# Two transfers, of 120 and of 8 partitions, in place of one of 128 for each quarter of the first weight matrix

## The chip, the cores and the metric

The kernel runs on one core of a Trainium2 chip. The metric is the device time of one execution in microseconds (us); the median of the runs of a kernel counts. Before the change three runs are there: 278.73, 279.89 and 282.72 us, median 279.89 us.

## What is computed

Causal retention with a decay per head, over 8 batches, 8 heads, 576 positions and a head size of 64; its output, laid out as 4608 tokens by 512, goes through two dense layers with a leaky ReLU between them.

```python
scores = scale * np.matmul(q, k.transpose(0, 1, 3, 2))
Dmat = np.where(rel >= 0, gamma[:, None, None] ** rel[None, :, :], 0.0)
attn_out = np.matmul(scores * Dmat[None, :, :, :], v)
x = attn_out.transpose(0, 2, 1, 3).reshape(4608, 512)
h = x @ w_in                      # 512 x 2048
g = np.maximum(0.01 * h, h)
out = g @ w_out                   # 2048 x 512
```

Inputs and output are float32.

## The kernel before, in words

**Units and groups.** The 4608 tokens are 36 units of 128 tokens (two chunks of 64 positions each), and four units make a group of 512 tokens, nine groups in all. Retention is done in chunks: inside a chunk by a masked product, across chunks by a running state per head.

**Names of the steps.** For unit u, `ld u.1`, `ld u.0` and `ld u.2` load k, q and v (line 340, tile `t`); a unit in which a batch ends is loaded by two transfers of 64 partitions each in place of one of 128. `ck`, `cq` and `cv` cast them to float16, q and v with the decay factors (lines 365 and 369). `tp` turns q and k on TensorE for the first eight units (L405) and `yt` copies them out (L412). `sa` and `sb` are the score and state products (L439, L448), `mk` the mask (L454), `st` the running state (L479 to L485), `sx` its float16 copy (L497, L500), `oa` or `ca`/`ow` the output products (L536), and `x u` copies the result into the group's `xT` (L585).

**The dense layers.** For groups 0 and 1 the first layer is done by plain products `h g.f0.t0` (L634: weights from `w_in`, moving data from `xT`), whose results pass through the leaky ReLU on ScalarE (`l`, L641). For the later groups both layers use seven products in place of eight on 2 by 2 blocks (L823 and L901), with sums of weight blocks (`ws`, L709, and `wm`, L680) and of activations made on VectorE. The stage of L634 runs until about 64 us of the span; after that nearly all of the time is the seven products.

**Weights.** `w_in16` is a float16 tile of 128 partitions by 4 by 2048. `load_w_in(f)`, line 602, loads quarter f (512 of the 2048 columns, all four blocks of 128 rows) with one transfer on the POOL queue, line 606, which casts float32 to float16 on the way: 128 partitions by 4 rows of 512 elements. `w_out16` is loaded by four such transfers, line 615. A product `h0.f0.t0` needs only the quarter that holds its columns: f0 = 0 to 3 need quarter 0, 4 to 7 quarter 1, 8 to 11 quarter 2, 12 to 15 quarter 3. The weight sums `ws` need all four quarters.

**What sets the order.** One string, `ORDER`, lists every step of the program; each engine and each queue carries out its own steps in that order. All loads up to unit 11, except k and q of unit 0, go through POOL, and so do the eight weight loads, so that they share one queue. Around the change the order of POOL's loads is (from `ORDER`, only the `ld`, `wi` and `wo` words):

```
ld2.1 ld3.0 ld3.1 wi0 ld4.0 ld3.2 wi1 ld4.1 ld5.1 ld4.2 ld5.2 wi2 ld6.2 ld5.0 ld6.1 wi3 ld7.2 ld7.1 ld8.1
ld6.0 ld8.2 ld7.0 ld9.1 ld9.2 wo0 wo2 wo1 wo3
```

Unit 4 is one that is loaded in halves, so `ld4.0`, `ld4.1` and `ld4.2` are two transfers each. The input tiles have four buffers for each of q, k and v. Words such as `+5@0` are products on an idle tile (L973) that keep TensorE going in the first 20 us.

Of the kernel before, what the change touches and what calls it, by code (L numbers as in the profile page):

```python
# [33 lines left out]
class Plan:  # L34
# [3 lines left out]
    def add(self, name, eng, run, after=(), opens=(), uses=(), mode="f"):  # L38
        j = Job(name, eng, run, [a for a in after if a is not None], list(opens), list(opens) + list(uses), mode)
        assert name not in self.jobs  # L40
        self.jobs[name] = j
        return j
# [169 lines left out]
def kernel(  # L212
# [9 lines left out]
    nc = tc.nc  # L222
# [2 lines left out]
    DFF = moe_w_in.shape[1]  # L225
    P = 128
    CH = 64
    BLK = 256
    NP = H // 2
    NF = DFF // P  # L230
# [2 lines left out]
    NU = NT // P  # L233
    CB = S // CH
    HF, HN, HT = NF // 2, DM // 2, TOK // 2
# [6 lines left out]
    def place(c):  # L242
        return (c % CB) % (BLK // CH)

    kinds = sorted({(place(2 * n), place(2 * n + 1)) for n in range(NU)})
    tab = np.zeros((P, len(kinds), 2, H))
    for w, at in enumerate(kinds):
        r = np.concatenate([CH * a + np.arange(CH) for a in at])[:, None] - BLK / 2
        tab[:, w, 0] = gamma[None, :] ** r * scale
        tab[:, w, 1] = gamma[None, :] ** (-r)  # L250
    s_idx = np.arange(P) % CH
    mask = (np.arange(CH)[None, :] >= s_idx[:, None]).astype(np.float32)
    gblk = np.zeros((P, NP))
    for p in range(NP):
        for g in range(2):
            gblk[CH * g : CH * g + CH, p] = gamma[p + NP * g] ** BLK
    consts = np.concatenate([tab.reshape(P, -1), mask, gblk], axis=1).astype(np.float32)
# [32 lines left out]
    w_in16 = const_pool.tile([P, NP, DFF], F16, name="w_in16")  # L290
# [138 lines left out]
    def inner(u):  # L429
# [39 lines left out]
        for j in range(2):  # L469
            if not live(u, j):  # L470
                carry[0] = None
                continue
            scaled = (2 * u + j) % CB % (BLK // CH) == BLK // CH - 1
            before = carry[0]
# [127 lines left out]
    def load_w_in(f):  # L602
        fs = slice(f * FQ, (f + 1) * FQ)

        def run():
            nc.gpsimd.dma_start(  # L606
                out=w_in16[:, :, fs], in_=moe_w_in.rearrange("(c k) f -> k c f", k=P)[:, :, fs]
            )

        w_in_job[f] = add(f"wi{f}", "POOL", run)  # L610
        follow(w_in_job[f])
# [365 lines left out]
    def follow(j):  # L977
        j.follow = last.get(j.eng)
        last[j.eng] = j
# [65 lines left out]
```

## Time and profile before

| what | value |
|---|---|
| median of 3 runs | 279.89 us (278.73 to 282.72) |
| the profiled execution's own time | 278.81 us |
| its span, first to last instruction | 277.0 us |
| mean granted TensorE clock | 0.997 of full speed |
| PE matmul, weight load, DVE, ACT, POOL busy | 97%, 81%, 84%, 70%, 14% |
| HBM read, written | 36.81 MB, 9.44 MB |

The profile is one execution. Its page gives the busy time of each engine (PE is the matrix engine, PEld its weight loads, DVE the vector engine, ACT the scalar engine, POOL the engine whose queue carries the casting transfers, SP the queue of the other transfers); the other views used are the timeline of one engine, the table of stretches with the busy time of each engine in each, the list of who waited for whom, the chain of work that ended last, and the view of one source line in a stretch, whose last row gives the time from the start of an issue to the landing of the data. In a timeline row stand the start, the length, the engine, the line, the operation with its tiles, the count, and in brackets the idle time of the engine before it with what ended it.

### The profile page before, as it was taken

How to read it: one execution, taken by the hardware profiler on the slowest of the kernel's cores; microseconds unless marked ns; L12 is line 12 of the kernel's file. 1: busy time of each engine (PE TensorE's matmuls, PEld its weight loads, DVE VectorE, ACT ScalarE, POOL GpSimd, SP SyncE). 2: the span in 40 equal slices, each digit the busy share in tenths (PEclk: the TensorE clock that was granted, in tenths of full speed). 3: DMA queues.
4: the chain of work that ended last, by engine and by line, in shares of the span. 5: the costliest groups of instructions: out<-in, count | busy, mean ns of one | idle time of the engine just before them, and what ended most of it. 6: DMA issues, size and time to landing. Idle time of an engine off the chain costs nothing.

```text
span 277.0 us, 10028 instructions
## 1 busy us (share of the span) xinstructions
PE 268.8 (97%) x4329; PEld 225.3 (81%) x4329; DVE 232.0 (84%) x438; ACT 195.2 (70%) x411; POOL 38.1 (14%) x49
## 2 busy tenths in 40 slices
PE   6999999999999999999999999999999999999994
PEld 2468668888888888888888888888898888888883
DVE  3888698979998999999989998999989968775650
ACT  2354596698889998798787889796769455447620
POOL 8958792200000000000000000000000000000000
PEclk9999999999999999999999999999999999999998
DMA  7999999987999999999999999998913700400404
GB/s 217 264 249 247 254 268 215 304 175 165 238 230 216 233 220 234 206 227 207 225 203 215 235 213 237 183 243 202 162 40 124 108 2 2 154 0 0 154 2 153
DMA packets 119597, 50.05 MB, mean 181 GB/s; under 512 B 107904, under 2 KB 113280, under 8 KB 119552
## 3 DMA queue, kind: packets, MB, share of 16 engines
q1 hardware_dynamic: 111984, 35.99, 60.3%
q0 software_dynamic: 6992, 13.11, 19.5%
q8 instruction: 34, 0.56, 0.8%
q10 hardware_dynamic: 576, 0.31, 0.4%
q14 instruction: 11, 0.09, 0.1%
HBM read 36.81 MB, written 9.44 MB: 167 GB/s over the span
## 4 chain that ended last, share of the span: by engine, by line
PE 88%; DMA 5%; POOL 3%; DVE 2%; issue 1%; ACT 0%; ACTq 0%; POOLq 0%; DVEq 0%
PE acc L901 40%; PE acc L823 31%; PE acc L634 9%; PE ot L536 4%; DMA t<-in_k_dram 3%; POOL t L340 2%; PE sc L448 2%; DMA t<-in_q_dram 2%; PE sc L439 2%; POOL w_in L606 1%; DVE osb L940 0%; PE acc L405 0%; DVE sum L847 0%; ACT acc L765 0%; DVE xT L585 0%
## 5 line engine op out<-in xcount | busy, mean ns | idle before, releaser
L901 PEld LDWEIGHTS <-gt 128*128 128x128 f16 x720 | 69.9, 98 | 8.3
L901 PE MATMUL acc<-w_out,gt 128*128 128x256 f16 x432 | 53.6, 273 | 0.0
L823 PEld LDWEIGHTS <-w_in 128*128 128x128 f16 x448 | 42.6, 98 | 5.8 <-issue 0.3
L843 ACT ACTIVATE gt<-acc 128x512 f16<-128x512 f32 x56 | 33.3, 601 | 13.7 <-PE acc L823 13.3
L901 PE MATMUL acc<-w_mix,gt 128*128 128x256 f16 x288 | 36.3, 273 | 0.0
L823 PEld LDWEIGHTS <-w_sum 128*128 128x128 f16 x336 | 32.3, 98 | 4.0
L851 ACT ACTIVATE gt<-sum 128x512 f16<-128x512 f32 x56 | 34.4, 635 | 1.1 <-DVE sum L847 0.9
L823 PE MATMUL acc<-xs,w_in 128*128 128x256 f16 x224 | 33.4, 273 | 0.3 <-ACT gt L843 0.3
L823 PE MATMUL acc<-xT,w_in 128*128 128x256 f16 x224 | 33.7, 273 | 0.0
L823 PE MATMUL acc<-xs,w_sum 128*128 128x256 f16 x224 | 33.7, 273 | 0.0
L901 PEld LDWEIGHTS <-mix 128*128 128x128 f16 x288 | 28.0, 98 | 3.8 <-DVE mix L877 0.4
L634 PE MATMUL acc<-xT,w_in 128*128 128x256 f16 (+2 forms) x272 | 30.3, 266 | 0.4 <-DVE xT L585 0.3
L454 DVE TENSOR_TENSOR s<-sc,cs 128x512 f16<-128x512 f32 x36 | 24.7, 685 | 5.7 <-PE sc L439 3.9
L634 PEld LDWEIGHTS <-w_in 128*128 128x128 f16 x272 | 22.0, 98 | 6.0 <-DMA w_in<-in_moe_w_in_dram 0.6
L641 ACT ACTIVATE gt<-acc 128x512 f16<-128x512 f32 x32 | 18.2, 599 | 10.2 <-PE acc L634 10.2
L762 ACT COPY acc<-acc 128x512 f32<-128x512 f32 x33 | 19.0, 577 | 8.8 <-PE acc L901 4.1
L847 DVE TENSOR_TENSOR sum<-acc,k 128x512 f32<-128x512 f32 x28 | 19.2, 688 | 6.6 <-ACT k L776 3.5
L369 DVE TENSOR_TENSOR qk<-t,cs 128x512 f16<-128x512 f32 x32 | 21.9, 683 | 1.0 <-DMA t<-in_q_dram 1.0
L585 ACT CAST xT<-ot 128x512 f16<-128x512 f32 x29 | 16.9, 591 | 8.1 <-PE ot L536 8.0
L776 ACT COPY k<-acc 128x512 f32<-128x512 f32 x31 | 18.3, 589 | 6.0 <-PE acc L823 3.6
L369 DVE TENSOR_TENSOR v<-t,cs 128x512 f16<-128x512 f32 x31 | 21.1, 684 | 0.4 <-PE ot L536 0.3
L847 DVE TENSOR_TENSOR sum<-acc,u 128x512 f32<-128x512 f32 x28 | 19.2, 686 | 2.4 <-PE acc L823 1.2
(64 smaller groups left out, 429.0 us busy)
## 6 DMA issues: line engine op xcount, KB each, us to landing
out_dram<-osb SPq DMA_DIRECT2D x16, 512.0 KB, 4.6
t<-in_k_dram SPq DMA_DIRECT2D x22, 256.0 KB, 4.3
t<-in_q_dram SPq DMA_DIRECT2D x22, 256.0 KB, 4.5
t<-in_v_dram SPq DMA_DIRECT2D x21, 256.0 KB, 4.0
t<-in_v_dram POOLq DMA_DIRECT2D x11, 256.0 KB, 5.9
t<-in_k_dram POOLq DMA_DIRECT2D x10, 256.0 KB, 8.1
t<-in_q_dram POOLq DMA_DIRECT2D x10, 256.0 KB, 6.5
w_in<-in_moe_w_in_dram POOLq DMA_DIRECT2D x4, 512.0 KB, 8.4
```

Of the source, the lines that this page charges most:

```text
L369: engine[e].tensor_tensor(out=view[0](out), in0=view[1](t32[u, 2 * x][:]), in1=view[1](decay(u, x)), op=MUL)
L454: landed[u] = nc.vector.tensor_tensor(out=s[:], in0=sc[:, :, 0], in1=mask_sb.unsqueeze(1).unsqueeze(1).to_broadcast([P, 2, NP, CH]), op=MUL,)
L585: moved[u] = copies[xe](out=x_of(u).rearrange("q c (j t) -> q j c t", j=2), in_=at)
L634: nc.tensor.matmul(out=a[:, n, :], lhsT=w_in16[:, c, (f0 + n) * P : (f0 + n + 1) * P], rhs=x[:, c, t0 : t0 + nt], start=(n == 0 and c == 0 ...
L641: nc.scalar.activation(out=y[:, f0 : f0 + nf, t0 : t0 + nt], in_=a[:], func=mybir.ActivationFunctionType.Lrelu)
L762: copies[ce](out=B[:], in_=A[:])
L776: op("k5", ke, lambda: copies[ke](out=k5[:], in_=C[:]), [done["5"]], [k5], [C])
L823: nc.tensor.matmul(out=r[:, f, :], lhsT=w[:, c, (2 * n + f) * P : (2 * n + f + 1) * P], rhs=rhs[:, c, :], start=fresh and c == 0 and f == ...
L843: w = op(what, "ACT", lambda: nc.scalar.activation(out=to(), in_=r[:], func=lr), after, [y], [r])
L847: what, "DVE", lambda: nc.vector.tensor_tensor(out=s[:], in0=r[:], in1=plus[:], op=ADD),
L851: f"l{g}.{n}.{what}", "ACT", lambda: nc.scalar.activation(out=to(), in_=s[:], func=lr), [j], [y],
L901: nc.tensor.matmul(out=(r[tb] if isinstance(r, tuple) else r)[:, tb, :], lhsT=lhs[n]()[:, f, tb * P : (tb + 1) * P], rhs=rhs[n][:, f, :], ...
```

## The change

`PW = 120` is added, and `load_w_in` issues two transfers in place of one, the first for partitions 0 to 119 and the second for partitions 120 to 127. Both stay on the POOL queue, next to each other, at the place in `ORDER` where the one stood. The steps that need a quarter need both of its parts. `load_w_out` stays as it is.

```diff
     P = 128
     CH = 64
+    PW = 120
...
         def run():
-            nc.gpsimd.dma_start(
-                out=w_in16[:, :, fs], in_=moe_w_in.rearrange("(c k) f -> k c f", k=P)[:, :, fs]
-            )
+            for ps in (slice(0, PW), slice(PW, P)):
+                nc.gpsimd.dma_start(
+                    out=w_in16[ps, :, fs], in_=moe_w_in.rearrange("(c k) f -> k c f", k=P)[ps, :, fs]
+                )
```

## The prediction, made before the changed kernel was run

> **What bounds the kernel now.** I read the page first, then the table of stretches, then the chain that ended last, then the queues that feed its start.
>
> ```profile
> span 277.0 us, 10028 instructions
> PE 268.8 (97%) x4329; PEld 225.3 (81%) x4329; DVE 232.0 (84%) x438; ACT 195.2 (70%) x411; POOL 38.1 (14%) x49
> ```
>
> TensorE is busy for 97% of the span. The question is where the remaining 3% lies and whether the loading of w_in has to do with it. Columns of the next table: stretch, its length, busy time of PE, PEld, DVE, ACT and POOL with counts, granted clock, mean busy share of the DMA engines, GB/s.
>
> ```profile
> 10.00:15.00 5.00, 4.86 (x79) 2.29 (x74) 4.82 (x10) 1.70 (x4) 5.00 (x8) 1.00 1.00 225
> 15.00:20.00 5.00, 4.71 (x119) 2.93 (x117) 4.28 (x11) 2.37 (x6) 2.08 (x4) 1.00 1.12 244
> 20.00:25.00 5.00, 4.89 (x130) 4.39 (x124) 3.43 (x8) 2.52 (x6) 3.85 (x5) 1.00 1.07 236
> 25.00:30.00 5.00, 4.56 (x103) 3.60 (x98) 3.73 (x9) 2.58 (x5) 5.00 (x7) 1.00 1.08 239
> 30.00:35.00 5.00, 5.00 (x91) 3.20 (x90) 3.90 (x9) 2.84 (x6) 3.11 (x5) 1.00 1.08 291
> 35.00:60.00 25.00, 25.00 (x363) 20.54 (x361) 23.11 (x44) 18.89 (x42) 10.08 (x12) 1.00 1.11 247
> ```
>
> From 30 to 60 us PE has no idle time. From 10 to 30 us, while the quarters of w_in are loaded, it lacks 0.14 + 0.29 + 0.11 + 0.44 = 0.98 us. That is the most that any faster loading of w_in can give back. The DMA share is 1.00 or more all the way (packets overlap), so the transfers run behind each other without a gap. Now the end of the start-up, from the chain of work that ended last, and the two places where PE's weight loads waited:
>
> ```profile
> 13.86 8.95 DMA t<-in_k_dram
> 25.86 0.69 DVE xT L585
> 26.61 1.96 PE acc L634 x32
> ```
> ```profile
> 18.42 0.91 PEld L634 LDWEIGHTS <-w_in 128*128 128x128 f16 x16 [0.61 <-DMA w_in<-in_moe_w_in_dram]
> 26.60 1.79 PEld L634 LDWEIGHTS <-w_in 128*128 128x128 f16 x32 [0.40 <-DVE xT L585]
> ```
> ```profile
> 22.90 0.76 DVE L365 CAST qk<-t 128x512 f16<-128x512 f32 x1 [0.98 <-DMA t<-in_k_dram]
> 23.91 0.65 DVE L365 CAST qk<-t 128x512 f16<-128x512 f32 x1
> ```
>
> The first wait is for quarter 0 itself. The second comes from the second half of k of unit 4, issued at 13.86 and landed at about 22.8: DVE stood 0.98 us before the cast at 22.90, and the copy x3 that PE needed at 26.60 is behind that cast on DVE. So two landings matter at first: quarter 0 at 18, k of unit 4 at 22.8. How POOL issues these:
>
> ```profile
> 9.30 0.77 POOL L606 DMA_DIRECT2D w_in<-in_moe_w_in_dram  x1
> 10.05 1.39 POOL L340 DMA_DIRECT2D t<-in_q_dram  x2
> 11.43 0.99 POOL L340 DMA_DIRECT2D t<-in_v_dram  x1
> 12.41 0.77 POOL L606 DMA_DIRECT2D w_in<-in_moe_w_in_dram  x1
> 13.16 2.28 POOL L340 DMA_DIRECT2D t<-in_k_dram  x3
> 18.36 2.26 POOL L340 DMA_DIRECT2D t<-in_v_dram  x3 [2.92 <-DMA w_in<-in_moe_w_in_dram]
> 20.61 0.77 POOL L606 DMA_DIRECT2D w_in<-in_moe_w_in_dram  x1
> 22.54 0.89 POOL L340 DMA_DIRECT2D t<-in_v_dram  x1 [1.15 <-DMA w_in<-in_moe_w_in_dram]
> ```
>
> Count the transfers between a quarter and the load that waits for it, although that load has nothing to do with w_in. After 9.30 come 2 + 1 + 1 + 3 = 7, and the eighth, at 18.36, waits. After 12.41 come 3 + 3 + 1 = 7, and the eighth, at 22.54, waits. I read this as a rotation: POOL's queue has eight transfers open, and the n-th waits until the one eight places before it has landed. The landings, from the views of the two lines in short stretches (quarters 0, 1, 2, then the second half of k4 with k5):
>
> ```profile
> L606 POOL DMA_DIRECT2D w_in<-in_moe_w_in_dram x1: 767/767/767, 9.3 to 9.3; - x1
> DMA to landing us min/median/max: 8.5/8.5/8.5
> ```
> ```profile
> L606 POOL DMA_DIRECT2D w_in<-in_moe_w_in_dram x1: 772/772/772, 12.4 to 12.4; - x1
> DMA to landing us min/median/max: 9.6/9.6/9.6
> ```
> ```profile
> L606 POOL DMA_DIRECT2D w_in<-in_moe_w_in_dram x1: 772/772/772, 20.6 to 20.6; - x1
> DMA to landing us min/median/max: 6.8/6.8/6.8
> ```
> ```profile
> L340 POOL DMA_DIRECT2D t<-in_k_dram x2: 697/799/901, 13.9 to 14.5; - x2
> DMA to landing us min/median/max: 8.9/9.1/9.3
> ```
>
> Quarter 0 lands at 9.30 + 8.5 = 17.8, quarter 1 at 22.0, quarter 2 at 27.4, k4's second half at 13.86 + 8.9 = 22.8, k5 at 14.5 + 9.3 = 23.8. Each waiting load starts 0.5 to 0.6 us after its landing (18.36 after 17.8, 22.54 after 22.0).
>
> **The change part by part.** *The issue.* Four more instructions stand on POOL. An 8-partition issue is not in the trace. The rows nearest to it are the 64-partition loads, 1.39 us for two (0.70 each), the 128-partition loads, 0.89 (2.26 for two halves and a whole), and w_in, 0.77. Carried on to 8 partitions on the line through the first two it is 0.70 - 56 x 0.19 / 64 = 0.53 us, which I take. It cannot be under zero, since the queue is in order and the issue takes time; its upper bound is the 0.77 of a whole quarter. Four cost +2.1 us of POOL (0 to 3.1); the 120-partition issue saves next to nothing. What hides it: POOL stands 2.92 and 1.15 us in the rows above, and the DMA engines are busy throughout. Without that cover two issues ahead of k4 would be +1.1 us. On the path: 0.
>
> *The packets.* The same bytes move. Their pace is seen while quarter 3 moves, from 28.7 to 30.9 us:
>
> ```profile
> DMA packets 353, 0.38 MB, mean 171 GB/s; under 512 B 3, under 2 KB 347, under 8 KB 353
> ```
>
> 353 packets in 2.2 us are 160 per us; a quarter has 128 x 4 = 512, so 3.2 us, or 32 packets of 0.10 us on each of 16 engines. If 120 partitions go 8 to an engine, fifteen engines get the same 32 and one gets none; the other 8 partitions are 32 packets more, 4 each if they spread over eight engines (+0.4 us there), or 3.2 us if one engine takes them (the engine left free, or one that then has 64). Bounds of quarter 0's landing: below, an engine that now ends late is freed; above, +0.4. A delay of 0.4 at 18.42 is swallowed by the 0.40 for which PE stands at 26.60. I take 0.
>
> The Trainium skill, "DMA: Bandwidth & Descriptors", section "Rules for kernel authors", speaks against such a split: two transfers of disjoint partitions use the same engines and serialize, so one of 128 is better. By it the sum would be that of one issue more and no gain, 0 to +0.4 here; the trace agrees so far that transfers queue behind each other (DMA share 1.00 to 1.12).
>
> *The rotation.* This is what the change moves. Quarter 0 takes two of the eight places, quarter 1 two as well. Counting again: q4 (two), v3, quarter 1 (two) and the first half of k4 follow quarter 0's small part; the second half of k4 is then the eighth after quarter 0's large part, and waits for it. It is issued at about 17.8 + 0.56 = 18.4 in place of 13.86, and k5 behind it at 19.1. Both were 8.9 and 9.3 us under way only because quarters were ahead. What a load needs with little ahead of it:
>
> ```profile
> t<-in_v_dram POOLq DMA_DIRECT2D x3, 256.0 KB, 4.4
> t<-in_k_dram POOLq DMA_DIRECT2D x3, 256.0 KB, 4.6
> t<-in_q_dram POOLq DMA_DIRECT2D x3, 256.0 KB, 4.2
> ```
>
> (medians of the loads issued before 9 us). So k4 lands between 18.4 + 4.2 = 22.6 and, with 4.6 and the 0.4 of packets, 23.4; now 22.8. k5: 19.1 + 4.2 to 5.0 = 23.3 to 24.1; now 23.8. I take no shift, because quarter 1 is still ahead and lands at 22.0. Quarter 2 is next: its large part stands eight places behind quarter 1's large part, so it starts at 22.0 + 0.56 = 22.6 in place of 20.61. With the same 6.8 it would land at 29.4; but part of the 6.8 was the queue, and v5, issued about 0.7 later than now, ends at about 25.7, which puts quarter 2 (2.5 us behind it now: 27.4 against 19.7 + 5.2) at 28.2 to 28.6. PE first uses it here:
>
> ```profile
> 28.94 2.76 PE L634 MATMUL acc<-xT,w_in 128*128 128x512 f16 x12
> ```
>
> That leaves 28.94 - 0.56 = 28.4 as its due time: from no cost to 29.4 - 28.4 = +1.0; I take 0, as it just fits.
>
> *Sum.* 0 + 0 + 0 against the profiled execution's 278.81 us (span 277.0 and 1.8 around it). That one lies 1.1 below the median of the runs shown, 279.89; on the median the forecast is **279.9 us**.
>
> **The rivals.**
>
> *A late engine is relieved.* A quarter has landed when the last engine is done. No view shows the engines apart. If the engine that carries partitions 120 to 127 is the one that ends late, it loses 32 packets, 3.2 us, per quarter, and quarter 0, k4 and k5 land earlier together. For it: 3.2 us of packets against landings of 6.8 to 9.6 leave room for an uneven end. Against it: the queue explains that too. Price: at most PE's 0.98 us, so 278.9. The Trainium skill's same page, section "Latency and other measured facts", says that engines 7 and 15 are usually slower, with a cause that it calls a best guess, and its section "Why a DMA increments its semaphore by 16 and not by 1" would put 120 partitions on engines 0 to 14 and so free 15. By these two the result would be this rival's 278.9; the trace can neither confirm nor deny which engine is late, so the chance stays small.
>
> *The rotation starves the engines: slower.* With k4's second half issued at 18.4, k5 at 19.1 and quarter 2 at 22.6, the queue runs dry. It decides if k4 takes more than 22.8 - 18.4 = 4.4 us from issue to landing. Price: k4 lands at 23.4, x3 and PE at 26.60 are 0.6 late; quarter 2 lands at 29.4 + 0.4 = 29.8, and PE starts on it at 30.3 in place of 28.94. The later wait contains the earlier: +1.3 to +1.4, 281.2 us. For it: the rotation, counted twice above. Against: 4.2 to 4.6 us for loads with an idle queue, and DMA at a share over 1.00.
>
> *Fewer engines than fifteen.* 120 is also 8 x 15; on eight engines a quarter is 60 packets, 6.0 us in place of 3.2. Four times 2.8 less about 1 us of slack is +10: 290 us. Against it: k4's half, 64 partitions, is 8.9 us under way beside 9.3 for all 128 of k5, so another count than 128 is not seen to slow a transfer.
>
> *It doesn't do what it says*, in that the 32 packets of the small part go to the one engine left free: then nothing changes but an issue, 279.9 as well; it is part of the forecast.
>
> **How the numbers follow.** Forecast 0.55 (own range 279.2 to 280.6), relief 0.21, rotation 0.20, fewer engines 0.04. The median of three runs can move by about 0.6 us by itself (half of 279.89 - 278.73), so the range is 278.9 - 0.6 = 278.3 to 281.2 + 0.6 = 281.8; outside are the 0.04 and the tails. A difference of 2%, 5.6 us, is about what a measurement of this kernel can tell from no change. Nothing reaches it on the fast side, since PE has 0.98 us to give; 0.01 for chance. Slower by it: the 0.04. Within: 0.95.
>
> **What would show it.** In the changed profile POOL should stand before the second k of unit 4, at about 15 to 18 us, and before the third large w_in issue; eight w_in issues, the small ones near 0.53 us. The cast of k4 on DVE should stay near 22.9, PE's L634 at 26.6 and 28.9, and PE idle from 10 to 30 us near 1 us. If quarter 0 lands by 17 and PE's wait at 18.42 goes, it is the relief; if the cast moves to 23.5 and PE waits for w_in near 29, the rotation. I am wrong if POOL's wait doesn't move to k4 (then there is no rotation of eight), or if PE shows new idle time after 30 us.

## The result, and the profile after the change

The changed kernel takes 283.31 us (median of 20 runs, 280.77 to 287.34) against 280.23 us of the kernel before (20 runs on the same chip, 278.3 to 283.76). The ratio is 1.0109, with a 95% interval of 1.0081 to 1.0138: slower by about 3 us. Two repetitions below gave 1.0062 and 1.0081, so that 2 to 3 us are a safer figure than 3.1. The profiled execution took 284.15 us.

The head of its page:

```profile
span 282.4 us, 10036 instructions
...
PE 268.7 (95%) x4329; PEld 224.8 (80%) x4329; DVE 232.5 (82%) x438; ACT 195.4 (69%) x411; POOL 40.6 (14%) x53
```

PE does the same work in the same time (268.7 us against 268.8), in a span that is 5.4 us longer: all of the loss is waiting. POOL has four instructions more (53 against 49) and 2.5 us more to do. The table of stretches shows where PE waits (columns as before; the last three are the granted clock, the DMA share and GB/s):

```profile
10.00:15.00 5.00, 4.69 (x101) 2.23 (x91) 4.80 (x11) 1.87 (x5) 5.00 (x8) 1.00 1.00 205
15.00:20.00 5.00, 3.73 (x98) 2.49 (x100) 3.56 (x10) 2.00 (x5) 1.75 (x4) 1.00 1.11 220
20.00:25.00 5.00, 3.82 (x115) 3.44 (x104) 2.23 (x5) 2.09 (x5) 3.13 (x5) 1.00 0.91 203
25.00:30.00 5.00, 4.60 (x117) 3.85 (x118) 4.08 (x10) 2.68 (x6) 5.00 (x7) 1.00 0.97 188
30.00:35.00 5.00, 4.92 (x124) 3.21 (x109) 3.74 (x8) 3.10 (x6) 4.96 (x6) 1.00 1.07 214
35.00:60.00 25.00, 24.09 (x356) 18.90 (x346) 22.76 (x43) 17.48 (x37) 11.85 (x15) 1.00 1.13 257
```

PE now lacks 0.31 + 1.27 + 1.18 + 0.40 + 0.08 + 0.91 = 4.15 us between 10 and 60 us, where it lacked 0.98. The DMA share, which was 1.00 or more in every stretch, is 0.91 and 0.97 from 20 to 30 us: there the DMA engines moved 203 and 188 GB/s in place of 236 and 239, as if short of work. Already from 10 to 20 us they moved less, 205 and 220 GB/s in place of 225 and 244, at nearly the same share; why is not shown. POOL's timeline:

```profile
9.28 1.40 POOL L608 DMA_DIRECT2D w_in<-in_moe_w_in_dram  x2
...
13.02 1.39 POOL L608 DMA_DIRECT2D w_in<-in_moe_w_in_dram  x2
14.40 0.73 POOL L341 DMA_DIRECT2D t<-in_k_dram  x1
18.37 1.62 POOL L341 DMA_DIRECT2D t<-in_k_dram  x2 [3.25 <-DMA w_in<-in_moe_w_in_dram]
...
24.12 1.39 POOL L608 DMA_DIRECT2D w_in<-in_moe_w_in_dram  x2 [1.58 <-DMA w_in<-in_moe_w_in_dram]
...
28.21 1.42 POOL L608 DMA_DIRECT2D w_in<-in_moe_w_in_dram  x2
```

POOL stands before the second half of k of unit 4 until 18.37, and before quarter 2 until 24.12 (20.61 before the change). The landings, from the view of line 608 in the short stretch of each issue: quarter 1's, quarter 2's and quarter 3's large part, each a view of its own.

```profile
L608 POOL DMA_DIRECT2D w_in<-in_moe_w_in_dram x1: 822/822/822, 13.0 to 13.0; - x1
...
DMA to landing us min/median/max: 10.8/10.8/10.8
```
```profile
L608 POOL DMA_DIRECT2D w_in<-in_moe_w_in_dram x1: 825/825/825, 24.1 to 24.1; - x1
...
DMA to landing us min/median/max: 5.9/5.9/5.9
```
```profile
L608 POOL DMA_DIRECT2D w_in<-in_moe_w_in_dram x1: 847/847/847, 28.2 to 28.2; - x1
...
DMA to landing us min/median/max: 8.4/8.4/8.4
```

The large part of quarter 1 lands at 13.02 + 10.8 = 23.8 (the whole quarter at 22.0 before), that of quarter 2 at 24.12 + 5.9 = 30.0 (27.4), that of quarter 3 at 28.21 + 8.4 = 36.6. The small parts land 0.2 to 0.25 us later, at 24.1, 30.25 and 36.8. Quarter 3 was not in the prediction's rows; in the kernel before it landed at 25.17 + 8.2 = 33.4, by the row

```profile
L606 POOL DMA_DIRECT2D w_in<-in_moe_w_in_dram x1: 767/767/767, 25.2 to 25.2; - x1
...
DMA to landing us min/median/max: 8.2/8.2/8.2
```

And PE's weight loads in the changed kernel:

```profile
18.59 0.91 PEld L636 LDWEIGHTS <-w_in 128*128 128x128 f16 x16 [1.57 <-DMA w_in<-in_moe_w_in_dram]
...
27.90 1.79 PEld L636 LDWEIGHTS <-w_in 128*128 128x128 f16 x32 [0.40 <-DVE xT L586]
30.36 2.29 PEld L636 LDWEIGHTS <-w_in 128*128 128x128 f16 x12 [0.16 <-issue]
...
36.95 2.29 PEld L636 LDWEIGHTS <-w_in 128*128 128x128 f16 x12 [1.38 <-DMA w_in<-in_moe_w_in_dram]
```

At 18.59 PE waits 1.57 us for quarter 0 (0.61 before); the products behind k4 start at 27.90 (26.60 before, with the same 0.40 behind VectorE); those on quarter 2 at 30.36, 0.1 us after its small part landed and with 0.16 us of waiting; and at 36.95 there is a wait of 1.38 us for quarter 3 that the kernel before has not. The chain that ended last runs from quarter 1's landing through POOL, which stood before quarter 2, to quarter 3; k of unit 4 is not in it. Four of its pieces:

```profile
13.02 10.80 DMA w_in<-in_moe_w_in_dram
25.51 1.53 POOL t L341 x2
29.02 7.83 DMA w_in<-in_moe_w_in_dram
36.98 2.75 PE acc L636 x12
```

PE's first product on quarter 3 (the 129th on w_in) starts at 36.98 in place of 34.47, and the first product of the second layer at 54.72 in place of 52.21 (PE's timeline): +2.5 us both times, which is what the runs show, 2 to 3 us. So in this execution the landing of quarter 3 sets the whole loss: PE's earlier waits are contained in it. The span of this one profile is 5.4 us longer because PE lacks another 2.2 us between 60 and 200 us (busy 137.50 in place of 139.67). The first repetition had 139.65 there with the same change and the second 138.01, so that it is not shown whether a part of those 2.2 us belongs to the change.

### The profile page after: what moved, and what is told of

Same layout as the page of the kernel before. It is cut to its first block, busy times and chain, and to the rows that moved or that the text cites. A ratio compares the mean times of both kernels' runs of the same rounds, so it can differ in the third digit from the quotient of the medians.

```text
span 282.4 us, 10036 instructions
## 1 busy us (share of the span) xinstructions
PE 268.7 (95%) x4329; PEld 224.8 (80%) x4329; DVE 232.5 (82%) x438; ACT 195.4 (69%) x411; POOL 40.6 (14%) x53
## 4 chain that ended last, share of the span: by engine, by line
PE 77%; DMA 13%; POOL 4%; ACT 3%; issue 1%; DVE 0%; ACTq 0%; POOLq 0%
PE acc L903 38%; PE acc L825 27%; DMA w_in<-in_moe_w_in_dram 7%; PE acc L636 6%; DMA qkT<-qk 5%; PE ot L537 3%; POOL t L341 3%; DMA t<-in_v_dram 2%; PE sc L449 1%; PE sc L440 1%; POOL w_in L608 1%; ACT gt L845 1%; ACT u L775 0%; ACT k L778 0%; ACT gt L853 0%
## 5 line engine op out<-in xcount | busy, mean ns | idle before, releaser
L903 PE MATMUL acc<-w_out,gt 128*128 128x256 f16 x432 | 53.6, 273 | 0.0
L825 PE MATMUL acc<-xT,w_in 128*128 128x256 f16 x224 | 33.7, 273 | 0.0
L825 PE MATMUL acc<-xs,w_in 128*128 128x256 f16 x224 | 33.4, 273 | 0.1
L643 ACT ACTIVATE gt<-acc 128x512 f16<-128x512 f32 x32 | 18.1, 597 | 13.3 <-PE acc L636 13.3
```

What stands on the lines that cost most here:

```text
L643: nc.scalar.activation(out=y[:, f0 : f0 + nf, t0 : t0 + nt], in_=a[:], func=mybir.ActivationFunctionType.Lrelu)
L825: nc.tensor.matmul(out=r[:, f, :], lhsT=w[:, c, (2 * n + f) * P : (2 * n + f + 1) * P], rhs=rhs[:, c, :], start=fresh and c == 0 and f == ...
L903: nc.tensor.matmul(out=(r[tb] if isinstance(r, tuple) else r)[:, tb, :], lhsT=lhs[n]()[:, f, tb * P : (tb + 1) * P], rhs=rhs[n][:, f, :], ...
```

## The experiments

Sixteen runs, of which e7, e16, e11, e12 and e13 repeat a kernel. Those that change only the split have the change's own lines with another `PW`. "Lacks" is the time that PE is not busy between 10 and 60 us of the one profile, "first" the start of the first product of the second layer. Landings are the last of the 16 counts with which a transfer reports that its engines are done; where a quarter needs two transfers, the later one.

| kernel | ratio (95%) | quarter 1 landed | quarter 2 issued, landed | quarter 3 landed | lacks | first |
|---|---|---|---|---|---|---|
| before; e13 again | | 22.0; 22.6 | 20.6, 27.4; 20.8, 28.2 | 33.4; 33.7 | 0.99; 2.33 | 52.2; 52.8 |
| the change, 120/8 | 1.0109 (1.0081 to 1.0138) | 24.1 | 24.1, 30.3 | 36.8 | 4.16 | 54.7 |
| e7 the change again | 1.0062 (1.0031 to 1.0093) | 23.7 | 23.8, 29.9 | 37.4 | 4.92 | 55.3 |
| e16 a third time | 1.0081 (1.0043 to 1.012) | 22.0 | 22.1, 29.0 | 34.6 | 2.90 | 54.9 |
| e14 104/24 | 1.0072 (1.0035 to 1.0109) | 23.5 | 23.4, 31.6 | 36.5 | | |
| e15 96/32 | 1.0036 (0.9998 to 1.0075) | 22.9 | 22.7, 28.4 | 34.5 | 1.62 | 53.1 |
| e5 112/16 | 1.0009 (0.9978 to 1.0041) | 23.2 | 23.3, 29.9 | 35.0 | 3.28 | 53.6 |
| e11 112/16 again | 1.0024 (0.9991 to 1.0056) | 22.0 | 22.0, 28.8 | 34.2 | 1.30 | 53.3 |
| e3 64/64 | 1.0029 (0.9994 to 1.0064) | 20.9 | 20.6, 27.7 | 33.0 | 0.73 | 52.1 |
| e4 120, the 8s by two quarters | 1.0027 (0.9996 to 1.0058) | 22.8 | 22.2, 29.5 | 34.2 | 3.04 | 53.5 |
| e12 the same again | 1.0043 (1.0015 to 1.0071) | 23.7 | 22.2, 30.5 | 36.0 | 3.35 | 54.2 |
| e9 112, the 16s by two | 1.0016 (0.9989 to 1.0044) | 22.6 | 21.0, 29.6 | 34.6 | 3.23 | 53.6 |
| e6 120/8, quarter 1 only | 1.0001 (0.9967 to 1.0034) | 22.4 | 22.5, 28.2 | 33.9 | 1.43 | 52.6 |
| e10 64/64, quarter 0 only | 0.9996 (0.9975 to 1.0018) | 21.5 | 20.2, 28.3 | 33.1 | 2.49 | 54.2 |
| e1 a spare transfer after quarter 1 | 1.0004 (0.9969 to 1.0038) | 21.5 | 21.8, 27.8 | 33.2 | 0.91 | 51.9 |
| e2 a spare one after quarter 0 | 0.9993 (0.9958 to 1.0029) | 21.7 | 21.2, 29.0 | 33.5 | 1.38 | 52.3 |

One profile is one execution: e13, the kernel before, lacks 2.33 us where its first profile lacks 0.99, and the two of 112/16 lack 3.28 and 1.30. So the ratios decide, and the profiles say where to look. The column "first" also holds stretches of a lower granted clock: 0.77 and 0.76 from 20 to 25 us in e4 and e12, 0.77 from 25 to 30 us in e10, 0.76 there in e16.

### The rotation alone: e1 and e2

A transfer of 2 KB that nothing needs takes one place of the eight, behind quarter 1 (e1) or quarter 0 (e2, `f == 0`). The bytes of the kernel and the shape of the quarters stay.

```diff
+    spare = const_pool.tile([8, D], FP, name="spare")
...
+            if f == 1:
+                nc.gpsimd.dma_start(out=spare, in_=q[0, 0, 0:8, :])
```

> The kernel before, with one transfer more on POOL: 2 KB into a tile that nothing reads, right behind quarter 1; the quarters stay whole. Rotation of eight: quarter 2 then waits for quarter 1, as in the changed kernel; POOL stands before quarter 2's issue until about 22.5 to 24, quarter 3 lands 1 to 3 us later than 33.4, and the time is up by 1 to 3 us (ratio 1.004 to 1.010). Shape (the 120 and 8 partitions themselves cost the time): nothing, 1.000. Issue time (0.6 us of POOL per issue): at most 0.6 us, 1.002.

> The same 2 KB transfer, right behind quarter 0 in place of quarter 1. Rotation: quarter 2 stays seven places and more behind quarter 1 and does not wait for it; only k5 now waits for quarter 0, so quarter 2 is issued within 1 us of the 20.6 of before, ratio 0.999 to 1.003, clearly under that of the transfer behind quarter 1. Shape: 1.000. Issue time: the same as behind quarter 1, at most 1.002.

POOL's timeline of e1:

```profile
13.25 0.54 POOL L611 DMA_DIRECT2D spare<-in_q_dram  x1
...
21.79 0.77 POOL L607 DMA_DIRECT2D w_in<-in_moe_w_in_dram  x1 [1.35 <-DMA spare<-in_q_dram]
```

The wait appears: quarter 2 is eight places behind the spare transfer, which lands in the queue behind quarter 1, and POOL stands 1.35 us before quarter 2. And it costs nothing: 1.0004, where the theory of the rotation called for +1 to +3 us (for e2 it called for nothing, and 0.9993 agrees). A stand before quarter 2 is not enough: issued at 21.8 and landed at 27.8 it is early enough. Nor is a stretch in which the DMA engines have little to do: from 20 to 25 us e1 has a lower DMA share (0.80) and fewer GB/s (172) than the changed kernel (0.91 and 203).

```profile
20.00:25.00 5.00, 4.75 (x128) 4.30 (x123) 3.94 (x9) 2.87 (x7) 3.65 (x5) 1.00 0.80 172
```

What e1 and e2 don't have is the stand before the second half of k4; in both POOL stands one load later, before k of unit 5 (issued at 17.2 and 18.1). Whole quarters with a stand at k4 and one at quarter 2 were not run. e2 settles one thing more: its quarter 1 was issued at 12.93 (12.41 before, 13.02 in the change) and landed at 21.7, so that half a microsecond of later issue does not by itself make quarter 1 late.

### One quarter alone: e6 and e10

```diff
-            for ps in (slice(0, PW), slice(PW, P)):
+            for ps in (slice(0, PW), slice(PW, P)) if f == 1 else (slice(0, P),):
```

e10 has `PW = 64` and `f == 0`.

> Only quarter 1 is split, 120 and 8; the other three stay whole. If the loss comes from quarter 2 waiting for a late quarter 1: quarter 1 lands 0.4 to 1.5 us later than the 21.5 to 22.0 of whole quarters, quarter 2 is issued at 22.5 to 23.5, ratio 1.002 to 1.006. If the loss adds up quarter by quarter: a quarter of it, 1.002 to 1.003, with quarter 2 not particularly late. If quarter 0's own landing (PE waits at 18) carries it: 1.000.

> Only quarter 0 is split, in 64 and 64 partitions; the others stay whole. In halves quarter 0 landed at 16.1 us against 17.8. If that landing and the wait behind it set the start: PE's waits at 18 and 26 us shrink, PE idle from 10 to 60 us 0.6 to 0.9, a gain of at most 0.4 us, ratio 0.997 to 1.000. If the shape of a split costs by itself: 1.001 to 1.003.

With quarter 1 alone split at 120, quarter 2 is issued at 22.5 after a wait of 1.01 us, lands at 28.2, and the time stays (1.0001). That misses the 1.002 to 1.006 of a loss by quarter 2's wait and the 1.002 to 1.003 of a loss that adds up by quarters; it is what was expected if quarter 0's landing carries the loss. Quarter 0 alone at 120 and 8 was not run, so that this is not decided. e10 had the first half of its quarter 0 at 15.8, but the whole at 17.3 and not at the 16.1 of e3, and showed 2.49 us of lacking PE time, where 0.6 to 0.9 was expected, with a ratio of 0.9996: a miss for the reading of single profiles.

### The shape of the split, same number of transfers: e3, e5, e11, e14, e15, and the change again: e7, e16

```diff
-    PW = 120
+    PW = 64
```

(112 in e5 and e11, 104 in e14, 96 in e15; e7 and e16 are the changed kernel itself.)

> The changed kernel with 64 and 64 partitions in place of 120 and 8: the same number of transfers, an even load of the engines. Rotation: the same loss as the change, ratio 1.008 to 1.013, POOL standing before the third quarter. Shape: the loss goes, 0.998 to 1.003. Issue time: the same loss as the change or a little more.

> The changed kernel with 112 and 16 partitions in place of 120 and 8: the same transfers in the same places, nearly the same sizes, but 112 and 16 both divide by 16, so that every engine gets 28 + 4 = 32 packets. Engine balance (120 leaves one engine without work and loads others more, and the rotation passes the late landing on): most of the loss goes, ratio 0.999 to 1.005, quarter 1 lands before 22.5. Any unequal split (a long part with a short one behind it): as the change, 1.008 to 1.013, quarter 1 near 23.8.

> 112 and 16 for all four quarters, again. Engine balance with the rotation still on: ratio 0.999 to 1.005 and PE idle from 10 to 60 us between the 1.0 of before and the 4.2 of the change. Any unequal split: as the change, 1.006 to 1.011, idle over 4.

> The changed kernel again, on the same chip as the others. All theories: ratio 1.008 to 1.014. In the profile: if the 2.9 us that the first profile lost after 55 us belong to the change, the transposing transfers again hold PE between 90 and 160 us and PE's idle time from 60 to 200 us is again 2 us and more above that of before; if they were chance, it is under 1 us, and the loss lies before 55 us.

> Split at 104 in place of 120, all four quarters, same count of transfers as the change. Theory A (an uneven split leaves some engine with a longer queue, so that the last engine ends a quarter late; 104 is no multiple of 16, as 120 is none): ratio 1.005 to 1.011, quarter 1 landed at 23.5 or later, POOL standing over 1 us before quarter 2, PE idle from 10 to 60 us 3 us or more. Theory B (it is the small last part of 8 partitions, a sixteenth of a quarter, and with 24 it is gone): 0.999 to 1.003, PE idle under 2 us.

> Split at 96, a multiple of 16 and of 32, same count of transfers as the change. Theories A and B both: 0.998 to 1.003, quarter 1 landed by 22.8, PE idle from 10 to 60 us 2 us or less. Theory C (any two transfers in a quarter with the second one smaller, by the rotation of eight places): 1.005 to 1.011, POOL standing over 1 us before quarter 2.

> The change a third time, beside the two other splits on one chip. All theories: ratio 1.004 to 1.011 (1.0109 and 1.0062 so far), quarter 1 landed at 23.3 to 24.2, PE idle from 10 to 60 us 4 to 5 us, first product of the second layer at 54.5 to 55.5.

All of these have eight w_in issues and the same places in the rotation. Where the first part is a multiple of 16 partitions (64, 96, 112), the ratio is 1.0009 to 1.0036, and all four intervals reach below 1. Where it is none (120 and 104) it is 1.0062 to 1.0109, and all four intervals lie above 1.003. e15 came out just above what was expected (0.998 to 1.003), and its interval overlaps that of e14; it is the set of eight that speaks, not that pair. e14's 1.0072 is within theory A's 1.005 to 1.011 and outside theory B's, so the 8 partitions of the last part are not the point; but POOL stood only 0.53 us before its quarter 2, not the 1 us and more that theory A expected. Of e14's profile only the loads are read, since that execution was the longest of its twelve.

The same places do not mean the same stands. Before quarter 2 POOL stands 1.58, 1.21 and 1.70 us in the three profiles of the change, 0.78 and 0.75 in e5 and e11, and not at all in e3 and next to nothing (0.04) in e15. But e5 and e11 also stand before the second half of k4, until 17.4 and 17.2, and cost 0.1 and 0.2%: the rotation, with its stands at both places, is not the whole cause. Two expectations were missed by a little: quarter 1 was to land before 22.5 in e5 (23.2), and e7 was to come out at 1.008 to 1.014 (1.0062).

What the two kinds of split do differently is seen in the counts of the trace. The 16 counts of quarter 2's first part, in us:

```
change, 120: 26.26 | 29.18 29.23 29.24 29.30 29.33 29.44 29.45 29.51 29.52 29.54 29.55 29.59 29.72 29.93 30.05
e14, 104:    25.49 25.86 26.00 | 28.51 28.67 28.72 28.77 28.79 28.80 28.82 28.85 28.87 28.89 28.90 29.09 31.19
e15, 96:     26.96 26.97 26.98 27.00 27.01 27.02 27.03 27.08 27.13 27.14 27.59 27.65 27.67 27.79 27.80 27.82
```

With 120 partitions one engine reports some 3 us ahead of the rest, with 104 three do, with 96 none: fifteen engines carry 8 partitions each, thirteen carry 8 each, sixteen carry 6 each. The Trainium skill, "DMA: Bandwidth & Descriptors", section "Why a DMA increments its semaphore by 16 and not by 1", says that the number of engines is the largest one up to 16 that divides the outermost size of both sides; that would be 15 for 120, 13 for 104, 16 for 96 and 112. The counts agree for 120, 104 and 96.

So with 120 or 104 the engines in use have as much to carry as for a whole quarter, and the small part comes on top on some of them; with 112, 96 or 64 the two parts add up to 8 partitions on each engine. That fits the ratios, but it is argued from these counts and not shown: with no more than that, 104 and 24 should be worse than 120 and 8, and it isn't.

e16 missed two of the three numbers expected of its profile (quarter 1 at 22.0, 2.90 us lacking) while its ratio and its first product, 54.9, were as expected. It has no wait for quarter 3, where e7 has 1.70 us. In that execution the granted clock was 0.76 from 25 to 30 us and 0.90 from 30 to 35, some 1.4 us of PE's time; how it would have gone at full clock can't be told.

### Fewer transfers at the same shape: e4, e12 and e9

The 8 partitions (16 in e9, `PW = 112`) of two quarters go in one transfer, behind quarters 0 and 2, so that the change adds two transfers in place of four, and quarter 2's large part is no longer eight places behind quarter 1's (its small part now is).

```diff
+            two = slice(f * FQ, (f + 2) * FQ)
+            for ps, cs_ in ((slice(0, PW), fs), (slice(PW, P), two))[: 2 - f % 2]:
...
-                    out=w_in16[ps, :, fs], in_=moe_w_in.rearrange("(c k) f -> k c f", k=P)[ps, :, fs]
+                    out=w_in16[ps, :, cs_], in_=moe_w_in.rearrange("(c k) f -> k c f", k=P)[ps, :, cs_]
```

> 120 partitions per quarter as in the change, but the 8 partitions of quarters 0 and 1 go in one transfer behind quarter 0's large part, those of quarters 2 and 3 behind quarter 2's: the same packets, two transfers more than before in place of four, and none more between quarter 1 and quarter 2. Rotation: quarter 2 does not wait for quarter 1 and is issued near 21; ratio 0.999 to 1.004. Shape: as the change, 1.008 to 1.013. Issue time: half of the change, 1.004 to 1.006.

> 120 partitions per quarter, small parts by two, again. Shape without the wait of quarter 2 for quarter 1: ratio 1.001 to 1.005, PE idle from 10 to 60 us 2 to 3.5, the longest wait on quarter 0 near 18 us. Shape alone carries all: 1.006 to 1.011, idle over 4.

> 112 partitions per quarter and the 16 left over of two quarters in one transfer, as in the kernel with the small parts by two: even packets per engine over the pair and no transfer more between quarter 1 and quarter 2. It is the fourth corner of a square: shape (120 or 112) by rotation (four or two transfers more). If shape and rotation each carry a part and add: PE idle from 10 to 60 us near the 1.0 us of before (under 1.8), ratio 0.998 to 1.002. If the loss is in any late short part behind quarter 0: idle 3 us, ratio 1.002 to 1.004.

POOL's timeline of e4 has quarter 2 issued with nothing waited for. The stand has moved from the second half of k4, issued at 14.52, to k of unit 5, the first row:

```profile
19.02 0.91 POOL L341 DMA_DIRECT2D t<-in_k_dram  x1 [3.83 <-DMA w_in<-in_moe_w_in_dram]
19.93 2.25 POOL L341 DMA_DIRECT2D t<-in_v_dram  x3
22.17 1.52 POOL L609 DMA_DIRECT2D w_in<-in_moe_w_in_dram  x2
```

At 120 the loss falls to 1.0027 and 1.0043, between a third and a half of the change's. So the places in the queue are a part of it; which of them is not separated, since the stand before k4 goes together with that before quarter 2, and quarter 2's small part still waits (0.13 us in e4, 0.95 in e12) and lands at 29.5 and 30.5. At 112 it is 1.0016, as with the full count (1.0009 and 1.0024). What is left at 120 without that wait begins at quarter 0, which landed at 18.7 and 18.8 in these two (17.8 and 18.0 in the kernel before, 18.5 and 18.1 in the change and e7); PE waited about 2.5 us for it. With quarter 0 later than in the change they lose less, so that quarter 0's landing does not carry the whole loss either. Of e9's two expectations the ratio fits the first (0.998 to 1.002) and the lacking time the second (3.23, where the first had less than 1.8).

### The shapes by themselves: e8

This kernel leaves out the whole computation: it loads the quarters of w_in over and over, in each of the shapes, and stores zeros. First one quarter at a time, each waiting for the one before, then the four quarters in a row.

```diff
+    shapes = ((whole,), (p120, p8), (p112, p16), (p64a, p64b))
+    for f in range(4):
+        for _ in range(3):
+            for parts in shapes:
+                for p in parts:
+                    p(f)
+    for _ in range(3):
+        for parts in shapes:
+            for f in range(4):
+                for p in parts:
+                    p(f)
```

> Leaves out the whole computation; it only loads quarters of w_in on POOL, first one shape at a time (each waits for the one before), then four quarters of one shape in a row, and stores zeros. Engine balance: alone, 120 and 8 take 0.3 to 0.6 us longer from first issue to last landing than 128 beyond the extra issue, and 112 and 16 do not; four in a row, 120 and 8 take 1.6 us more than 128 (36 packets in place of 32 on eight engines), 112 and 16 and 64 and 64 at most 0.6. Any split costs: all three the same. Packets slower in the long part: 120 itself takes over 0.5 us longer than 112.

One at a time, POOL's timeline (L228 is the whole quarter, L231 and L234 are 120 and 8, L237 and L240 112 and 16, L243 the first of the halves):

```profile
39.81 0.78 POOL L228 DMA_DIRECT2D w_in<-in_moe_w_in_dram  x1 [9.11 <-DMA w_in<-in_moe_w_in_dram]
45.66 0.80 POOL L231 DMA_DIRECT2D w_in<-in_moe_w_in_dram  x1 [5.07 <-DMA w_in<-in_moe_w_in_dram]
46.46 0.56 POOL L234 DMA_DIRECT2D w_in<-in_moe_w_in_dram  x1
51.42 0.72 POOL L237 DMA_DIRECT2D w_in<-in_moe_w_in_dram  x1 [4.40 <-DMA w_in<-in_moe_w_in_dram]
52.13 0.52 POOL L240 DMA_DIRECT2D w_in<-in_moe_w_in_dram  x1
56.94 0.62 POOL L243 DMA_DIRECT2D w_in<-in_moe_w_in_dram  x1 [4.29 <-DMA w_in<-in_moe_w_in_dram]
```

From the first issue to the last landing the median is 5.33 us for a whole quarter (5.19 to 5.56 in eight), 5.88 for 120 and 8 (5.70 to 6.09 in eleven), 5.67 for 112 and 16 (5.63 to 5.76) and 5.01 for the halves (4.84 to 5.86). The 0.55 us by which 120 and 8 take longer than the whole are no more than the second issue, 0.56, so that the 0.3 to 0.6 us beyond the extra issue which the theory of the busiest engine called for are not there. Against 112 and 16, which also have a second issue, they take 0.2 us longer.

In a row, each block of four quarters is measured from the last landing of the block ahead of it to its own. Four quarters of 120 and 8 took 11.05, 11.13 and 10.24 us in the three rounds, whole ones 10.09 and 10.38 (the first block of whole ones had nothing ahead of it), 112 and 16 10.14, 10.08 and 10.84, the halves 10.29, 10.21 and 9.64. The theory called for 1.6 us more over four quarters. Two rounds of three have 0.7 to 1.0 more and the third has none, so that as a price it missed; that the uneven shape is a little slower in a full queue is neither shown nor excluded.

### The kernel before again: e13

> The kernel before, unchanged, for the chance of one profile. All theories: 278.5 to 281.5 us; PE idle from 10 to 60 us 0.7 to 1.6 us (0.99 in its first profile); quarter 2 issued at 20.5 to 21.0; first product of the second layer at 51.9 to 52.6. If the idle time comes out at 2 us or more, the profiles of the experiments can't be ranked by it, and the ratios alone decide.

279.8 us, and the row of its table for the whole stretch:

```profile
10.00:60.00 50.00, 47.67 (x859) 36.01 (x859) 42.96 (x86) 30.18 (x64) 28.94 (x36) 1.00 1.11 246
```

50 - 47.67 = 2.33 us lacking, above the 0.7 to 1.6 that was expected, and the second layer starts at 52.8, just past the 51.9 to 52.6: the idle time of single profiles is not fit for ranking, as the expectation said of this case.

## Why the prediction was right or wrong

The forecast was no change, 279.9 us. The kernel became slower by 0.6 to 1.1%.

**What bounds the kernel: right.** PE had about 1 us to gain, nothing was gained, and what was lost is PE's waiting in the same stage.

**The issues on POOL: right.** The small issue was taken at 0.53 us, and the pairs take 1.40 where one took 0.77, 0.6 more each; alone it is 0.56 (e8). That it is hidden fits e2, where a spare issue ahead of quarter 1 cost nothing.

**The rotation of eight: right, and where it strikes too.** POOL stands at k4's second half (predicted at about 18.4, measured at 18.37) and before quarter 2. e1 shows it by itself with a transfer that is put in. One of the prediction's own signs of being wrong came true, though: PE has new idle time after 30 us.

**The price of the rotation: wrong, and this is the step that failed.** It was taken as no shift, and the term that was mis-sized is the landing of quarter 1. The prediction held it at 22.0, for k4 ("I take no shift, because quarter 1 is still ahead and lands at 22.0") and for quarter 2 ("it starts at 22.0 + 0.56 = 22.6"). In the change's profile it was 24.1 (23.7 and 22.0 in e7 and e16), and both terms moved with it. The first is k4, which was to land between 22.6 and 23.4. The rows of its two halves, each from the view of line 341 at that issue:

```profile
L341 POOL DMA_DIRECT2D t<-in_k_dram x1: 726/726/726, 14.4 to 14.4; - x1
...
DMA to landing us min/median/max: 9.9/9.9/9.9
```
```profile
L341 POOL DMA_DIRECT2D t<-in_k_dram x1: 697/697/697, 18.4 to 18.4; - x1
...
DMA to landing us min/median/max: 6.3/6.3/6.3
```

The second half took 6.3 us and not 4.2 to 4.6: it landed at 24.7, VectorE cast it at 24.76, and PE's products at 26.60 went to 27.90. But the first half, which waited for nothing and went out right behind quarter 1, landed at 24.3 as well (22.25 before). In all seventeen profiles of the full kernel the second half lands 0.5 to 1.3 us after quarter 1, whether it was issued at 13.8 or at 18.4. So the stand before k4, on which the prediction spent its sum, hardly moves k4; quarter 1 does. The rows of an idle queue were the wrong ones for a load that is issued behind a quarter. The second term is quarter 2, which started at 24.12 in place of 22.6. Its large part landed at 30.0, past the due time of 28.4 by 1.6 us: it did not "just fit". PE, late by k4, stood only 0.16 us for it; its price comes with quarter 3, which is issued behind it on POOL and which the sum left out.

**Quarter 0: too small.** Up to 0.4 us was allowed, to be swallowed by the 0.40 for which PE stands behind VectorE. In the change's profile PE's wait grew from 0.61 to 1.57, and the 0.40 was still there at 27.90, since k4 had moved as well. The 0.61 is not all quarter 0's, as the prediction read it: PE's weight loads stand 0.61 us there in e3 and e16 too, with quarter 0 landed at 16.1 and 15.6.

**The rival of the rotation: its mechanism at its places, priced a step too short.** It had k4's chain 0.6 late (measured 1.3) and PE starting on quarter 2 at 30.3 (measured 30.36). That agreement is in part luck: the rival had quarter 2 as what PE waits for there, and of the 1.4 us 1.3 are k4's. There it ended, at +1.3 to +1.4. It didn't ask what is late next: quarter 3 is issued behind quarter 2, at 28.21 in place of 25.17, lands whole at 36.8 in place of 33.4, and PE waits until 36.95 for it. That later wait contains the earlier ones and is the +2.5: 3.4 us of lateness, less the 1.06 us by which quarter 3 was early before (landed at 33.41, used at 34.47), and 0.14 from its landing to PE's start. But the experiments also correct this rival: standing at the queue is not enough. e1 and e6 stand 1.35 and 1.01 us before quarter 2, issue it at 21.8 and 22.5, and lose nothing. In the change's profile it costs because quarter 1 itself lands late. That this comes with the uneven split is likely and not shown by the landings: quarter 1 lands at 22.0 to 24.1 in the profiles with 120 or 104 and at 20.9 to 23.2 in the others, ranges that overlap.

**The relief of a late engine: wrong.** One engine has no part in the 120 partitions, as the counts show, but the last of the others lands no earlier: quarter 0's large part at 18.1 against 17.8 and the whole quarter 1 at 24.1 against 22.0. In e16 quarter 0 did land early, at 15.6, which was the rival's sign, and that kernel was slower all the same (1.0081). No run shows which engine is late or which one is left out, nor that it is the same one each time, so that the guess about slower engines is neither borne out nor refuted by name.

**Fewer engines than fifteen: wrong**, by the same counts.

**What stays open.** Shown: in the change's profile a row of late quarters, with the wait for quarter 3 as the last; and, by the set of ratios, that splits at 120 or 104 lose where splits at 64, 96 or 112 with the same number of transfers lose little or nothing. Shown in part: fewer transfers in the queue take away half of the loss or somewhat more at 120 (e4 and e12 against the change, with intervals that overlap in part). Not shown: why the quarters land late with the uneven split, and whether quarter 0's split alone would do it. Uneven queues of the single engines, with the last of them setting each landing, are the likely reason; 104 against 120 doesn't confirm it, and e8 has it in two rounds of three.

## What to carry to other kernels

When a transfer is split, count what stands a fixed number of places behind it in its queue, and price the load that comes late with rows of loads that had the same traffic ahead of them; then go on to the next load in the queue until one has slack, since here the last late quarter set the whole loss. Check the landing that such a sum holds fixed: here it was quarter 1's. If a split is wanted at all, cut at a multiple of 16 partitions: in this kernel those splits cost 0.1 to 0.4%, with intervals that include no loss, and the others 0.6 to 1.1%. At differences below 1% one profile can't rank two versions here: the same kernel lacked 0.99 us in one execution and 2.33 in another.

## What the runs showed of the hardware that was not expected

Alone, splitting a quarter into halves mostly brings it in sooner: in e8 the last count came 5.01 us after the first issue (median of eleven, eight of them at 4.84 to 5.17) against 5.33 for the whole (5.19 to 5.56), and each of the two issues costs 0.62 in place of one of 0.78. In the full kernel, e3's quarter 1 landed at 20.9 (22.0 and 22.6 before), and the time didn't fall: 1.0029, PE having nothing to gain. The Trainium skill, "DMA: Bandwidth & Descriptors", section "Rules for kernel authors", says of two transfers of disjoint halves of the partitions not to bother, since they serialize. For the time of this kernel the runs agree; for the landing by itself they do not.

An issue of 8 or 16 partitions costs POOL 0.51 to 0.57 us in e8 against 0.78 for 128, so that most of it doesn't depend on the size.
